# GFNet mixing and an MLP by Winograd doubles: ten plain steps and 31 doubles in place of twelve and 30, and the token sums begun earlier

## The chip, the cores and the metric

The kernel runs on one core of a Trainium2 chip. The metric is the device time of one launch in microseconds (us), the median of several runs.

## The reference, cut to what matters

```python
def _A_ref(x, w_r, w_i):                 # S = 2048 tokens, D = 576
    X = rfft2(x) * (w_r + 1j * w_i)
    return irfft2(X, (S, D))

def _B_ref(x, w1, w2):                   # Dff = 4608
    h = maximum(einsum("bsd,df->bsf", x, w1), 0)
    return einsum("bsf,fd->bsd", h, w2)

h = x + _A_ref(_layernorm(x), w_r, w_i)
out = h + _B_ref(_layernorm(h), w1, w2)  # all float32
```

## The kernel before, in words

The first part does the two-dimensional transform as matmuls, multiplies by the complex weight, transforms back, adds the residual and normalises again. A projection step `j` (function `project`) transposes one tile of 128 normalised tokens and writes it to the token chunk's tile `xc` and to DRAM (`xd`). The rest of the time, from about 150 us on, is the MLP.

Every float32 operand is held as a high part (rounded by ScalarE, "split" and `act`) and a low part (the difference, by VectorE or GpSimd), and each product is three matmuls: high by high, high by low, low by high. The 4608 hidden units are 18 groups of 256, the 2048 tokens are 4 chunks of 512 (of 4 tiles of 128).

The MLP has two kinds of work. A **plain step** (group, chunk) is `mm1` (2 halves of 14 matmuls of 512 columns) and `mm2` (4 token tiles of 12 matmuls of 288 columns, each followed by an add of VectorE onto the residual, L625). Between them stands `relu_split`: ScalarE makes the high part (L631), VectorE the low part (L632). A **double** (group, p) does one group for the two chunks of pair p by the Strassen-Winograd scheme: 7 first products (`l1_prod`, 7 matmuls of 512 columns, L816) and 14 second products (`second` and `prod`, 6 matmuls of 288 columns, L921). It needs sums of the weights (GpSimd makes them, `w1_sums` and `w2_sums`), sums of the hidden values (`piece`), and sums T1 to T4 of the two chunks of tokens. These **token sums** are the same for every group, so they are made once, by `sum_jobs`: for each pair p and tile j the four loads from `xd`, four subtractions (two of VectorE, L678 and L679, two of GpSimd, L680 and L681), the high parts (ScalarE), the low parts (VectorE, L672 for columns and L673 for the 32 leftover rows). They pass through two staging buffers (`stage`) to DRAM (`keep`), and `load_sum` brings them back to the chunks' tiles when a double wants them, since both pairs' sums don't fit beside each other.

The order is written out by hand and each engine runs its queue in that order. SP issues nearly all DMAs in program order. `STEPS` orders the projections with the first plain steps; then a loop over i runs `mm1(i + 1, q)` and `mm2(i, q)` in quarters (i, q), and behind each quarter a job of `sum_jobs`. The last plain step END is woven into the first double's first products. After it each `slot(d)` weaves the first products of double d + 1 with the second products of double d. Slots alternate: one prepares the next group's W1 (its parts A11, S12, S34: `weights`), the other, with `turn` set, prepares A2 and W2 and streams the other pair's sums in (`STREAM`).

All four banks `ps()` of the plain loop's PSUM are handed out in a ring: each `mm1` pair and each `mm2` tile takes the next one, so that TensorE waits when VectorE has not read the bank of three or four pieces before.

Of the kernel before, what the change touches and what calls it, by code (L numbers as in the profile page):

```python
# [129 lines left out]
def kernel(ctx: ExitStack, tc: tile.TileContext, x, w_r, w_i, w1, w2, cc2, c1, fb, ib, c3, out):  # L130
# [518 lines left out]
    def sum_jobs(p, j):  # L649

        fs = FT[j % 2]
        b11, b12, b21, t2, b22 = (fs[k > 1][:, 384 * k - 768 * (k > 1):384 * k - 768 * (k > 1) + 384] for k in range(5))
        v3 = lambda v, a=3: v.rearrange("p (a n) -> p a n", a=a)
# [8 lines left out]

        def high(k):
            f = fs[k][:, :768].rearrange("p (m a n) -> p m a n", m=2, a=3)
            o = stage[k].rearrange("p (m a n) -> p m a n", m=2, a=5)
            for m in range(2):
                act(o[:, m, 0:3], f[:, m])

        def low(k):
            f = fs[k][:, :768].rearrange("p (m a n) -> p m a n", m=2, a=3)  # L670
            o = stage[k].rearrange("p (m a n) -> p m a n", m=2, a=5)
            nc.vector.tensor_sub(o[:, :, 3:5], f[:, :, 0:2], o[:, :, 0:2])  # L672
            nc.vector.tensor_sub(o[64:96, :, 2], f[64:96, :, 2], o[64:96, :, 2])  # L673
            for m, n_ in enumerate((("T1", "T3"), ("T4", "T2"))[k]):
                keep(p, n_, (640 * j, stage[k][:, 640 * m:640 * m + 640]))

        def sums_():
            nc.vector.tensor_sub(b11, b12, b11)  # L678
            nc.vector.tensor_sub(t2, b22, b11)  # L679
            nc.gpsimd.tensor_sub(b12, b22, b12)  # L680
            nc.gpsimd.tensor_sub(b21, b21, t2)  # L681

        def highs():
            high(0)
            high(1)

        def lows():
            low(0)
            low(1)

        return load, sums_, highs, lows
# [475 lines left out]
```

## Time and profile before

| | |
|---|---|
| median of 3 runs | 975.83 us (975.36 to 976.69) |
| the profiled execution's own time | 975.89 us |
| its span | 974.1 us |
| granted TensorE clock, mean | 0.999 |
| TensorE busy | 961.8 us, 99% of the span |
| VectorE, ScalarE, GpSimd busy | 753.8, 454.3, 607.0 us |
| data moved | 178.71 MB, mean 183 GB/s |

The own time is 1.8 us longer than the span, which holds only what the profiler recorded of the engines. Busy time is that of the engines' instructions; TensorE's matmuls are pipelined, so a start-to-start distance says more than a duration of one.

### The profile page before, as it was taken

The page shows a single profiled execution, that of the slowest core. Times are in us where ns is not written, and L with a number is a line of the kernel's source. Part 1 is how long each engine was busy: PE and PEld are TensorE (multiplying, and loading weights), DVE is VectorE, ACT ScalarE, POOL GpSimd, SP SyncE. Part 2 cuts the span into 40 slices and gives each one's busy share as a digit, 9 for nine tenths or more (in the row PEclk, how much of TensorE's full clock was granted, in tenths as well). Part 3 has the DMA queues.
Part 4 walks back from the last instruction along what each step waited for, and adds up shares of the span by engine and source line. Part 5 has one row for each costly group of instructions (what it writes and reads, how often), then busy time and mean ns, then how long its engine had stood idle before and what let it go on. Part 6 is the DMA issues. An engine that isn't in the chain of part 4 may idle for free.

```text
span 974.1 us, 18067 instructions
## 1 busy us (share of the span) xinstructions
PE 961.8 (99%) x6677; PEld 852.9 (88%) x6677; DVE 753.8 (77%) x1190; ACT 454.3 (47%) x887; POOL 607.0 (62%) x740
## 2 busy tenths in 40 slices
PE   8999999999999999999999999999999999999997
PEld 7777678899988899999999999999999999999997
DVE  8677977357665888888888887888887888888886
ACT  6544556223244445445454454444454544544441
POOL 7213756312265777777786868776777868687741
PEclk9999999999999999999999999999999999999999
DMA  7874724647697292735537281927355472819365
GB/s 217 228 178 118 174 96 135 215 146 243 225 345 273 69 313 64 262 125 200 183 142 241 85 299 36 313 63 262 124 201 182 144 251 74 298 36 315 110 209 146
DMA packets 124247, 178.71 MB, mean 183 GB/s; under 512 B 7936, under 2 KB 102784, under 8 KB 124160
## 3 DMA queue, kind: packets, MB, share of 16 engines
q1 hardware_dynamic: 123424, 176.68, 56.0%
q8 instruction: 53, 0.87, 0.4%
q10 hardware_dynamic: 736, 0.89, 0.3%
q14 instruction: 34, 0.28, 0.1%
HBM read 153.15 MB, written 23.07 MB: 181 GB/s over the span
## 4 chain that ended last, share of the span: by engine, by line
PE 92%; DVE 5%; DMA 1%; issue 1%; ACT 0%; SPq 0%; POOL 0%; DVEq 0%; POOLq 0%
PE h L816 34%; PE w L921 33%; PE d L156 23%; DMA B<-t1T 1%; DVE A L519 1%; DVE st L215 1%; PE d L564 1%; DVE st L242 1%; DVE A L931 0%; DVE e L536 0%; DVE e L537 0%; DMA X<-in_A_x_dram 0%; PE w L156 0%; PE h L921 0%; ACT X L159 0%
## 5 line engine op out<-in xcount | busy, mean ns | idle before, releaser
L931 DVE TENSOR_TENSOR A<-A,w 128x576 f32<-128x576 f32 x415 | 308.1, 752 | 81.3 <-PE w L921 68.7
L921 PE MATMUL w<-X,D 128*128 128x288 f32 x1416 | 214.9, 294 | 0.1
L921 PEld LDWEIGHTS w<-X,D 128*128 128x128 f32 x1416 | 202.5, 188 | 10.0 <-DVE A L931 0.3
L816 PE MATMUL h<-B,e 128*128 128x512 f32 x630 | 160.1, 393 | 1.2 <-DVE A L625 0.6
L159 ACT ACTIVATE e<-h 128x512 f32<-128x512 f32 x90 | 53.8, 598 | 181.8 <-PE h L816 181.8
L816 PEld LDWEIGHTS h<-B,e 128*128 128x128 f32 x630 | 113.2, 188 | 21.2 <-DMA B<-t1T 0.9
L353 POOL TENSOR_TENSOR e<-e,e 128x512 fp32r<-128x512 f32 (+3 forms) x62 | 81.2, 1309 | 45.9 <-ACT e L159 45.7
L816 PE MATMUL h<-X,e 128*128 128x512 f32 x420 | 106.5, 393 | 0.0
L635 ACT ACTIVATE e<-e 128x512 f32<-128x512 f32 x90 | 56.9, 632 | 104.2 <-DVE e L874 44.7
L353 POOL TENSOR_TENSOR X<-e,X 128x576 fp32r<-128x576 f32 (+1 forms) x32 | 47.2, 1476 | 71.5 <-ACT X L159 71.5
L816 PEld LDWEIGHTS h<-X,e 128*128 128x128 f32 x420 | 75.5, 188 | 13.0
L159 ACT ACTIVATE e<-e 128x256 fp32r<-128x256 f32 (+4 forms) x162 | 74.5, 489 | 24.7 <-DVE e L678 11.1
L840 POOL TENSOR_TENSOR A<-e 128x256 f32<-128x256 f32 x59 | 46.6, 789 | 27.7 <-DVE X L830 24.6
L830 DVE TENSOR_TENSOR D<-A,D 128x512 fp32r<-128x512 f32 x59 | 61.4, 1041 | 0.9 <-ACT D L159 0.9
L921 PEld LDWEIGHTS w<-X 128*128 128x128 f32 x360 | 53.8, 188 | 5.5 <-issue 0.7
L921 PE MATMUL w<-X 128*128 128x288 f32 x360 | 57.0, 294 | 0.5 <-DVE A L931 0.5
L921 PE MATMUL w<-X,e 128*128 128x288 f32 x348 | 55.2, 294 | 0.0
L156 PE MATMUL d<-e,D 128*128 128x288 f32 x384 | 53.6, 295 | 0.0
L816 PE MATMUL h<-C,e 128*128 128x512 f32 x210 | 53.2, 392 | 0.0
L816 PE MATMUL h<-F,e 128*128 128x512 f32 x210 | 53.2, 392 | 0.0
L156 PEld LDWEIGHTS d<-e,D 128*128 128x128 f32 x384 | 51.9, 188 | 1.3 <-issue 0.4
L842 POOL TENSOR_TENSOR A<-e,A 128x256 f32<-128x256 f32 x59 | 51.4, 871 | 0.8 <-DVE A L838 0.8
(168 smaller groups left out, 1863.2 us busy)
## 6 DMA issues: line engine op xcount, KB each, us to landing
X<-t0T SPq DMA_DIRECT2D x16, 768.0 KB, 8.4
X<-t1T SPq DMA_DIRECT2D x16, 768.0 KB, 8.1
e<-in_B_w_dram SPq DMA_DIRECT2D x18, 576.0 KB, 4.3
e<-in_B_w_dram SPq DMA_DIRECT2D x18, 512.0 KB, 3.8
X<-t0T SPq DMA_DIRECT2D x16, 512.0 KB, 8.6
X<-t1T SPq DMA_DIRECT2D x16, 512.0 KB
B<-t0T SPq DMA_DIRECT2D x8, 768.0 KB
F<-t0T SPq DMA_DIRECT2D x8, 768.0 KB
```

The lines of the kernel that those rows point to most:

```text
L156: nc.tensor.matmul(o, l, r, start=start, stop=stop)
L159: nc.scalar.activation(o, i, AF.Copy, **kw)
L215: nc.vector.bn_stats(st[:, i, h, :], xs[:, t0 + i, 288 * h:288 * h + 288])
L242: nc.vector.bn_stats(first(t)[2][:, h, :], xs[:, t, 288 * h:288 * h + 288])
L353: eng.tensor_sub(l, v, h)
L635: nc.scalar.activation(o, i, AF.Relu)
L816: nc.tensor.matmul(o, a, b, start=bool(first) and n_ == 0, stop=n_ == len(ops) - 1, skip_group_check=not first)
L830: (eng or nc.vector).tensor_sub(f[1], v, f[0])
L840: nc.gpsimd.tensor_sub(s3, p0[:, :256], p0[:, 256:])
L842: nc.gpsimd.tensor_sub(s4, p1_[:, :256], s2)
L921: nc.tensor.matmul(P[tt], l[:, q], r, start=first and n_ == 0, stop=end and n_ == 2, skip_group_check=whole and not first)
L931: nc.vector.tensor_add(xt, xt, P)
```

## The change

There are ten plain steps (groups 0 and 1, and two of group 2) and FIRST is 2: the first double is group 2 for pair 0, and the doubles of groups 3 to 17 follow, 31 in all. The raw weights of group 2 are loaded once, for the plain steps and for the double; before, group 2's were loaded for the plain steps and group 3's for the first double. The first slot now is a `turn` slot, and group 3's W1 is prepared during END (`weights(-1, r)`, with VectorE in GpSimd's place for the low parts).

The token sums are begun during the last projections: loads (=L), subtractions (=S), high (=H) and low parts (=W) stand among the steps, and the rest is dealt by hand over 18 quarters (`JOBS`, quarters (3, 0) to (7, 1)). Their inputs land in a region of the big tile instead of in buffer F. T1 and T4 of pair 0 are written where the doubles read them, and not through `stage`; they are stored to DRAM later, in END (`load_sum(0, "T1", True)`), since the pair's sums are streamed in again later. The low parts are four pairs of instructions of half the size in place of two. A31 stands ahead of B20 in `STEPS`.

```diff
--- before.py
+++ after.py
@@ -582,8 +582,8 @@
...
-    steps = [(0, 0), (0, 1), (0, 2), (1, 1), (0, 3), (1, 3), (1, 0), (1, 2), (2, 3), (2, 1), (2, 0), (2, 2)]
-    FIRST = 3
+    steps = [(0, 0), (0, 1), (0, 2), (1, 1), (0, 3), (1, 3), (1, 0), (1, 2), (2, 3), (2, 2)]
+    FIRST = 2
     END = len(steps) - 1
 
...
+    def sum_jobs(p, j, place):
+
+        part = lambda v, k: v[:, 384 * k:384 * k + 384]
+        i0 = 7680 + 1536 * (j % 2)
+        b11, b21, b12, b22 = (tail[0][:, i0 + 384 * k:i0 + 384 * k + 384].bitcast(F32) for k in range(4))
+        outs, terms, parts = {}, {}, {}
 
         def load():
-            for t, (x, y) in ((8 * p + j, (b11, b21)), (8 * p + 4 + j, (b12, b22))):
-                nc.sync.dma_start(x[:, :256], xd[t][:, :256])
-                nc.sync.dma_start(y[:, :256], xd[t][:, 384:])
-                for h, v in enumerate((x, y)):
-                    o, i = v[:, 256:], xd[t][32 * h:32 * h + 32, 256:384]
-                    nc.sync.dma_start(o, bass.AP(tensor=i.tensor, offset=i.offset, ap=[[0, 4], list(i.ap[0]), [1, 128]]))
+            q = nc.sync
...
+        def sums_():
+            t1, t3, t4, t2 = (part(v, k) for v, k in FT[place])
+            nc.vector.tensor_sub(t1, b12, b11)
+            nc.vector.tensor_sub(t2, b22, t1)
+            nc.gpsimd.tensor_sub(t3, b22, b12)
+            nc.gpsimd.tensor_sub(t4, b21, t2)
+            terms.update(T1=t1, T3=t3, T4=t4, T2=t2)
 
...
+            for m, n_ in enumerate((("T1", "T3"), ("T4", "T2"))[k]):
+                if p == 0 and not m:
+                    hi, lo = (v.rearrange("p a n -> p (a n)").rearrange("p (j a n) -> p j a n", j=4, n=128)[:, j] for v in TF[n_])
+                else:
+                    stage.append(stage.pop(0))
+                    outs[n_] = stage[-1]
+                    o = outs[n_].rearrange("p (a n) -> p a n", a=5)
+                    hi, lo = o[:, :3], o[:, 3:]
+                parts[n_] = hi, lo, terms[n_].rearrange("p (a n) -> p a n", a=3)
+                act(hi, parts[n_][2])
 
...
+            for n_ in (("T1", "T3"), ("T4", "T2"))[k]:
+                hi, lo, v = parts[n_]
+                nc.vector.tensor_sub(lo, v[:, :2], hi[:, :2])
+                nc.vector.tensor_sub(hi[64:96, 2], v[64:96, 2], hi[64:96, 2])
+                if n_ in outs:
+                    keep(p, n_, (640 * j, outs[n_]))
+
+        return dict(L=load, S=sums_, H=lambda: high(0), I=lambda: high(1), W=lambda: low(0), X=lambda: low(1))
 
...
-    def load_sum(p, n):
+    def load_sum(p, n, back=False):
+        if back:
+            td[p, n] = dram.tile([128, 2560], F32, name=f"t{p}{n}")
...
+            nc.sync.dma_start(*((t, v) if back else (v, t)))
 
...
-    doubles = [(g, p) for g in range(FIRST, NG) for p in ((0, 1) if g % 2 == FIRST % 2 else (1, 0))]
+    doubles = [(FIRST, 0)] + [(g, p) for g in range(FIRST + 1, NG) for p in ((1, 0) if g % 2 == FIRST % 2 else (0, 1))]
     LAST = len(doubles) - 1
 
...
-        return [wps[8 - 2 * bank + k][:, :288] for k in range(2)]
+        return [wps[4 + k if bank == 2 else 2 + (k + LAST + 1) % 2][:, :288] for k in range(2)]
 
...
-        g, p = doubles[d]
-        turn = d % 2
-        if not turn and r == 0 and d:
+        g = doubles[max(d, 0)][0]
+        turn = (d + 1) % 2
+        eng = nc.vector if d < 0 else nc.gpsimd
+        if not turn and r == 0 and d > 0:
             w2_split("T34", nc.vector)
             w2_split("B22", nc.gpsimd)
         if g == NG - 1:
@@ -976,20 +980,22 @@
...
             for n_, k in STREAM:
-                if k == r:
+                if max(k, 2 * (d == 0)) == r:
                     load_sum(doubles[d + 2][1], n_)
         else:
+            if r == (1 if d > 0 else 5):
+                load_w2(g + 1, vs[2])
             if r == 1:
-                load_w2(g + 1, vs[2])
-                w1_split("A11", nc.gpsimd)
-            if r == 2:
+                w1_split("A11", eng)
+            early = d < 0
+            if r == 2 - early:
                 w1_sums(0)
-            if r == 3:
+            if r == 3 - early:
                 w1_sums(1)
-            if r == 4:
-                w1_split("S12", nc.gpsimd)
-            if r == 5:
-                w1_split("S34", nc.gpsimd)
+            if r == 4 - early:
+                w1_split("S12", eng)
+            if r == 5 + early:
+                w1_split("S34", eng)
 
...
-        "B12 n14 B13 j12 V0 A20 j13 V1 A21 j14 A30 j15 B20 B21 A31 B22 B23 "
+        "B12 n14 B13 j12 V0 =L0 =L1 A20 j13 V1 =P0 A21 =S0 j14 A30 =S1 j15 =L2 =L3 A31 B20 =P1 B21 =H0 B22 =W0 =H1 B23 =W1 =S2 "
     )
 
...
+        groups.extend(sum_jobs(k // CH, k % CH, v) for k, v in enumerate("ABCABABA"))
+
+    groups, stage, FT = [], [], {}
+
+    def keep_block(p):
+        keep(p, "B22", *((at, v.rearrange("p a n -> p (a n)")) for at, v in zip((0, 1536), khalf(2 * p + 1, 1))))
+
...
+    JOBS = (
+        "L4 / H2 I0 I1 / W2 X0 X1 / S3 L5 I2 / X2 H3 I3 / W3 X3 K1 / S4 L6 / "
+        "H4 I4 / W4 X4 / S5 L7 / H5 I5 / W5 X5 / S6 / H6 I6 / W6 X6 / S7 / H7 I7 / W7 X7"
+    ).split(" / ")
+
...
+    def work(k):
+        for v in JOBS[k].split() if 0 <= k < len(JOBS) else ():
+            job(v[0], int(v[1:]))
 
...
     for i in range(3, END):
         if i == 3:
-            load_weights(2, leftover())
-        if i == 8:
-            vs[1], vs[2], vs[4] = ebuf([128, 4, 256]), ebuf([128, 2, D]), leftover()
-            load_w1(FIRST, vs[1], vs[4])
-            load_w2(FIRST, vs[2])
-        if i == 8:
-            TF.update(T1=khalf(1, 0), B22=khalf(1, 1), T2=khalf(3, 0), T3=khalf(3, 1))
+            TF.update(B22=khalf(1, 1), T2=khalf(3, 0), T3=khalf(3, 1))
         for q in range(4):
             if q < 2:
                 mm1(i + 1, q)
             mm2(i, q)
-            if i == 3 and q == 1:
...
+            if (i, q) == (3, 1):
+                TS = sb([128, 5, 512], "F", dt=F32R)
+                TF["T4"] = TS[:, 0:3], TS[:, 3:5]
+            work(4 * i + q - 12)
+            if (i, q) == (4, 3):
+                load_weights(FIRST, leftover())
+                vs[1], vs[2], vs[4] = raw[FIRST]
+            if (i, q) in ((5, 3), (7, 1)):
+                split_weights(FIRST, i > 5)
+            for n_, k in (("T2", (7, 1)), ("T3", (7, 2))):
                 if k == (i, q):
                     load_sum(doubles[0][1], n_)
...
+            if (i, q) == (END - 2, 2):
...
                 w2_sums()
-            if (i, q) in ((9, 3), (10, 0)):
+            if (i, q) in ((END - 2, 3), (END - 1, 0)):
                 w2_split(("T34", "T12")[q == 3], nc.gpsimd)
...
-                        w1_split(n_, nc.vector if n_ == "A11" else nc.gpsimd)
+                        w1_split(n_, nc.vector if n_ == "A2" else nc.gpsimd)
...
     for i in (END,):
         load_w1(FIRST + 1, vs[1], vs[4])
+        load_sum(0, "T1", True)
...
-            for n_, k in STREAM:
-                if k == r:
-                    load_sum(doubles[1][1], n_)
+            if r == 5:
+                load_sum(0, "T4", True)
+            weights(-1, r)
```

Three places show how the rows move. The first is VectorE behind `mm2(7, 1)`, with the split of group 2's second weight (L353, 128x4x288) that `mm2(8, 0)` reads. The letters are tiles: A the residual, e and F buffers, X the big tile, d a PSUM bank. Before:

```order
L625 TENSOR_TENSOR A_1396<-A_1396,d_3018 128x576
L672 TENSOR_TENSOR e_2463<-F_2541,e_2463 128x2x256
L673 TENSOR_TENSOR e_2463<-F_2541,e_2463 32x2x128
L672 TENSOR_TENSOR e_2464<-F_2541,e_2464 128x2x256
L673 TENSOR_TENSOR e_2464<-F_2541,e_2464 32x2x128
L353 TENSOR_TENSOR X_2146<-e_2474,X_2146 128x4x288
L625 TENSOR_TENSOR A_1396<-A_1396,d_3046 128x576
```

And in the changed kernel (the left-out rows repeat the pair ahead of them):

```order
L625 TENSOR_TENSOR A_1396<-A_1396,d_3090 128x576
L687 TENSOR_TENSOR e_2460<-A_1396,e_2460 128x256
L688 TENSOR_TENSOR e_2460<-A_1396,e_2460 32x128
...
L687 TENSOR_TENSOR e_2461<-e_2339,e_2461 128x256
L688 TENSOR_TENSOR e_2461<-e_2339,e_2461 32x128
...
L353 TENSOR_TENSOR X_2149<-e_2781,X_2149 128x4x288
L625 TENSOR_TENSOR A_1396<-A_1396,d_3120 128x576
```

Four low parts stood ahead of the split, and now eight do (a pair for each of T1 to T4).

The second place is VectorE at the end of the first double and the start of slot 0, up to the add that frees the bank of the first second-product (w, L931). Before:

```order
L874 TENSOR_TENSOR e_3413<-e_3413,h_3476 128x512
L882 TENSOR_TENSOR e_3413<-e_3413,h_3477 128x512
L830 TENSOR_TENSOR X_2146<-e_3413,X_2146 128x256
L836 TENSOR_TENSOR A_1396<-e_3413,e_3501 128x256
L838 TENSOR_TENSOR A_1396<-A_1396,e_3413 128x256
L830 TENSOR_TENSOR D_3479<-A_1396,D_3479 128x512
L353 TENSOR_TENSOR e_3410<-e_3413,e_3617 128x256
L931 TENSOR_TENSOR A_1396<-A_1396,w_3615 128x2x288
```

And now (lines are three higher from `load_sum` on, L934 is the add):

```order
L877 TENSOR_TENSOR e_3229<-e_3229,h_3295 128x512
L885 TENSOR_TENSOR e_3229<-e_3229,h_3296 128x512
L833 TENSOR_TENSOR X_2149<-e_3229,X_2149 128x256
L839 TENSOR_TENSOR A_1396<-e_3229,e_3320 128x256
L841 TENSOR_TENSOR A_1396<-A_1396,e_3229 128x256
L353 TENSOR_TENSOR e_3225<-e_3136,e_3225 128x512
L377 TENSOR_TENSOR e_3227<-e_3229,e_3227 32x256
L833 TENSOR_TENSOR D_3298<-A_1396,D_3298 128x512
L353 TENSOR_TENSOR e_3226<-e_3229,e_3450 128x256
L934 TENSOR_TENSOR A_1396<-A_1396,w_3448 128x2x288
```

The two low parts of group 3's S34 (L353 128x512 and L377) have moved in ahead of the low part of the hidden sums (L833, D) and of the add.

The third place is SP in END, from the load of group 3's W1 on (e and G are raw weights, t0T and t1T the stored sums of pairs 0 and 1). Before:

```order
L333 DMA e_3090<-in_B_w_dram 128x4x256
L335 DMA G_3092<-in_B_w_dram 32x2x256 x3
L706 DMA X_2146<-t1T_3042 128x4x384
L706 DMA X_2146<-t1T_3042 128x4x256
L706 DMA B_1413<-t1T_3034 128x4x384
L706 DMA B_1413<-t1T_3034 128x4x256
```

And now:

```order
L333 DMA e_2780<-in_B_w_dram 128x4x256
L335 DMA G_2778<-in_B_w_dram 32x2x256 x3
L709 DMA t0T_3286<-B_1413 512x1x384
L709 DMA t0T_3286<-B_1413 512x1x256
L709 DMA t0T_3433<-F_2590 512x1x384
L709 DMA t0T_3433<-F_2590 512x1x256
L343 DMA e_2781<-in_B_w_dram 128x2x576
```

The loads of pair 1's T2 and T1 have left this place, since the second double now is of pair 0 too; two sums of pair 0 are stored in their stead.

## Rows read from the trace of the kernel before

**Rows 1.** The page, busy time of each engine.

```profile
PE 961.8 (99%) x6677; PEld 852.9 (88%) x6677; DVE 753.8 (77%) x1190; ACT 454.3 (47%) x887; POOL 607.0 (62%) x740
```

**Rows 2.** Windows of 25 us: busy per engine, clock, DMA share, GB/s.

```profile
core 0: us, PE busy (x) PEld busy (x) DVE busy (x) ACT busy (x) POOL busy (x), PEclk, DMA share, GB/s
...
225.00:250.00 25.00, 25.00 (x151) 22.61 (x149) 17.31 (x28) 9.89 (x17) 5.82 (x6) 1.00 0.58 195
...
275.00:300.00 25.00, 24.36 (x141) 21.66 (x140) 12.04 (x18) 9.61 (x19) 19.51 (x24) 1.00 0.80 292
```

**Rows 3.** Waits of TensorE: engine, line, releaser: us, times, longest.

```profile
PE h L816 <- DVE A L625: 0.6, 1, 0.6
PE h L816 <- DMA B<-t1T: 0.6, 1, 0.6
```

**Rows 4.** Timeline of TensorE, plain steps: start us, us, line, operation.

```profile
186.59 3.38 PE L156 MATMUL d<-X,F 128*128 128x512 f32 x14
...
194.62 4.90 PE L156 MATMUL d<-e,D 128*128 128x288 f32 x36
...
275.92 3.38 PE L156 MATMUL d<-C,e 128*128 128x512 f32 x14
```

**Rows 5.** Chain that ended last, in order of time, two doubles' beginnings.

```profile
806.08 1.62 PE h L816 x7
...
828.42 1.60 PE h L816 x7
```

**Rows 6.** Timeline of TensorE, first double and slot 0.

```profile
289.47 1.85 PE L816 MATMUL h<-B,e 128*128 128x512 f32 x7 [0.64 <-DVE A L625]
...
310.47 1.65 PE L816 MATMUL h<-B,e 128*128 128x512 f32 x6 [0.60 <-DMA B<-t1T]
311.96 1.75 PE L921 MATMUL w<-X,D 128*128 128x288 f32 x12
```

**Rows 7.** Timeline of VectorE, first double and slot 0.

```profile
292.94 0.75 DVE L625 TENSOR_TENSOR A<-A,w 128x576 f32<-128x576 f32 x1 [3.61 <-PE w L156]
299.33 0.76 DVE L625 TENSOR_TENSOR A<-A,w 128x576 f32<-128x576 f32 x1 [5.63 <-PE w L156]
...
309.46 0.43 DVE L838 TENSOR_TENSOR A<-A,e 128x256 f32<-128x256 f32 x1
310.58 0.69 DVE L830 TENSOR_TENSOR D<-A,D 128x512 fp32r<-128x512 f32 x1 [0.70 <-ACT D L159]
311.19 0.42 DVE L353 TENSOR_TENSOR e<-e,e 128x256 fp32r<-128x256 f32 x1
311.53 0.75 DVE L931 TENSOR_TENSOR A<-A,w 128x576 f32<-128x576 f32 x1
```

**Rows 8.** Timeline of VectorE, behind mm2(7, 1).

```profile
248.72 0.69 DVE L672 TENSOR_TENSOR e<-F,e 128x512 fp32r<-128x512 f32 x1
249.42 0.42 DVE L673 TENSOR_TENSOR e<-F,e 32x256 fp32r<-32x256 f32 x1
...
251.02 1.36 DVE L353 TENSOR_TENSOR X<-e,X 128x1152 fp32r<-128x1152 f32 x1
```

**Rows 9.** Timeline of TensorE, first mm2 of step 8.

```profile
253.62 1.74 PE L156 MATMUL d<-X,D 128*128 128x288 f32 x12
```

**Rows 10.** Timelines of VectorE and GpSimd near 282 us.

```profile
282.35 1.57 DVE L673 TENSOR_TENSOR e<-e,e 32x256 fp32r<-32x256 f32 x1
...
282.21 3.01 POOL L353 TENSOR_TENSOR X<-e,X 128x576 fp32r<-128x576 f32 x2 [2.64 <-ACT X L159]
```

**Rows 11.** Timelines of VectorE and ScalarE: a relu's second half; a high part.

```profile
234.16 1.22 DVE L632 SCALAR_TENSOR_TENSOR D<-d,D 128x1024 fp32r<-128x1024 f32 x1 [1.89 <-ACT D L631]
...
241.95 0.53 ACT L159 ACTIVATE e<-F 128x384 fp32r<-128x384 f32 x1 [6.18 <-DMA t0T<-e]
```

**Rows 12.** DMA issues 150 to 330 us; one window of 10 us.

```profile
t1T<-e SPq DMA_DIRECT2D x16, 320.0 KB, 6.7
...
280.00:290.00 10.00, 9.36 (x59) 8.49 (x58) 8.62 (x12) 5.45 (x12) 7.63 (x10) 1.00 1.06 384
```

More of the change, by code (lines that the diff above doesn't have):

```diff
@@ L647, in keep @@
             nc.sync.dma_start(td[p, n][:, at:at + v.shape[1]], v.bitcast(F32))
[L649 to L653, printed above, removed]
-        def load():
-            for t, (x, y) in ((8 * p + j, (b11, b21)), (8 * p + 4 + j, (b12, b22))):
-                nc.sync.dma_start(x[:, :256], xd[t][:, :256])
-                nc.sync.dma_start(y[:, :256], xd[t][:, 384:])
-                for h, v in enumerate((x, y)):
-                    o, i = v[:, 256:], xd[t][32 * h:32 * h + 32, 256:384]
-                    nc.sync.dma_start(o, bass.AP(tensor=i.tensor, offset=i.offset, ap=[[0, 4], list(i.ap[0]), [1, 128]]))
-        def high(k):
[L664 to L667, printed above, removed]
-        def low(k):
[L670 to L691, printed above, removed]
@@ L1055, in tail_in, with sum_bufs, job @@
         load_weights(1, v4)
+        groups.extend(sum_jobs(k // CH, k % CH, v) for k, v in enumerate("ABCABABA"))
+    groups, stage, FT = [], [], {}
+    def keep_block(p):
+        keep(p, "B22", *((at, v.rearrange("p a n -> p (a n)")) for at, v in zip((0, 1536), khalf(2 * p + 1, 1))))
+    def sum_bufs(k):
+        if k == 0:
+            a, b = (ebuf([128, 1152]) for _ in range(2))
+            FT.update(A=((sums, 0), (sums, 1), (a, 0), (a, 1)), B=((b, 0), (b, 1), (b, 2), (a, 2)))
+            TF["T1"] = khalf(1, 0)
+        if k == 1:
+            c = ebuf([128, 1152])
+            FT["C"] = (c, 0), (c, 1), (c, 2), (sb([128, 512], "G"), 0)
+            for _ in range(2):
+                v = ebuf([128, 1280], F32R)
+                stage.extend((v[:, :640], v[:, 640:]))
+    JOBS = (
+        "L4 / H2 I0 I1 / W2 X0 X1 / S3 L5 I2 / X2 H3 I3 / W3 X3 K1 / S4 L6 / "
+        "H4 I4 / W4 X4 / S5 L7 / H5 I5 / W5 X5 / S6 / H6 I6 / W6 X6 / S7 / H7 I7 / W7 X7"
+    ).split(" / ")
+    def job(name, k):
+        if name in "LSHIWX":
+            groups[k][name]()
+        else:
+            dict(K=keep_block, P=sum_bufs)[name](k)
+    def work(k):
+        for v in JOBS[k].split() if 0 <= k < len(JOBS) else ():
+            job(v[0], int(v[1:]))
     CALLS = dict(h=inv_h, d=inv_d, o=inv_o, r=inv_r, e=inv_e, s=stat2, n=lambda t: norm2(t, 2), j=project,
@@ L1060 @@
     for step in STEPS.split():
-        CALLS[step[0]](int(step[1:] or 0))
-    stage = [ebuf([128, 1280], F32R) for _ in range(2)]
-    for p in range(2):
-        keep(p, "B22", *((at, v.rearrange("p a n -> p (a n)")) for at, v in zip((0, 1536), khalf(2 * p + 1, 1))))
-    jobs = []
+        if step[0] == "=":
+            job(step[1], int(step[2:]))
+        else:
+            CALLS[step[0]](int(step[1:] or 0))
     fx = {}
@@ L1103 @@
                 w2_sums()
-            if (i, q) in ((9, 3), (10, 0)):
+            if (i, q) in ((END - 2, 3), (END - 1, 0)):
                 w2_split(("T34", "T12")[q == 3], nc.gpsimd)
-            if i == 10:
+            if i == END - 1:
                 if q == 0:
```

31 lines of the change are left out of this document (9 added, 22 removed), and 2 rows, old and new, of the table STEPS.

## The prediction

> **What bounds the kernel now.** I read the page first: TensorE is busy for 99% of the span and the next engine, VectorE, for 77% [rows 1]. So nearly every microsecond less of matmuls is one less of time, if the other engines keep pace; and what they can lose is little, because they have slack only between the deadlines that TensorE sets. Next the windows of 25 us. In the plain loop (225 to 250 us) TensorE has no idle at all, at a granted clock of 1.00 (the 2.4 GHz level), and VectorE has 7.7 us of 25 free; TensorE's first gap of size lies between 275 and 300 us, 0.64 us [rows 2]. Then the waits: the two long ones in the part that changes are 0.6 us for a VectorE add and 0.6 us for the load of a token sum [rows 3]. The timeline puts the first at the beginning of the first double, where the residual adds of the last plain steps come late (0.64), and the second in slot 0, where T1 of pair 1 has not landed (0.60) [rows 6].
>
> **Two plain steps less, one double more.** The start of a plain step's `mm1` stands at 186.59 and, seven steps later, at 275.92 [rows 4]: 89.33 / 7 = 12.76 us a step, 25.52 for two. A double is seven pairs of pieces, 806.08 to 828.42, with nothing between them: 22.34 us [rows 5]. It does seven eighths of the products of two plain steps, and 25.52 x 7/8 = 22.33 agrees. The exchange is worth 22.34 - 25.52 = **-3.18 us** on TensorE. It holds only where TensorE stays fed, since nothing was idle there before.
>
> **The token sums.** The eight groups of sums are made between the last projections and step 7, where they took steps 3 to 9 before. The low parts are eight instructions a group in place of four, each of half the size. Those of 128x256 take 0.42 us (the L353 row at 311.19) [rows 7]. No row has VectorE at 32x128: above it stands 32x256 at 0.42 [rows 8], below it nothing; I take 0.3, nearer to the row, since halving 128x512 took it only from 0.69 to 0.42. A group then costs 4 x 0.42 + 4 x 0.3 = 2.9 us (1.7 to 3.4) where it cost 2 x (0.69 + 0.42) = 2.2. Eight groups: 5 us more of VectorE, against 7.7 free in each 25. On average that is hidden; what counts is what stands behind the lows in the queue. Two places are tight.
>
> The first is `mm2(8, 0)`. Its third matmul reads the low part of group 2's second weight. Before, that split started at 251.02 and ended at 252.38 [rows 8]; TensorE began at 253.62 and wanted the low part two matmuls of twelve later, at 253.9 [rows 9]. Step 8 keeps its clock time, for what is removed comes later. Now eight lows stand ahead, so the split ends at about 252.38 + 0.66 = 253.0, with 0.9 in hand, if nothing holds it. But right behind it the program has GpSimd's weight sums and the low parts T34, which stood two steps later before. Where these two kinds met, a 32x256 low of VectorE took 1.57 us in place of 0.42, inside a pair of GpSimd lows of 3.01 [rows 10]: 1.15 us lost to one meeting. One meeting puts the split's end at 254.2, a wait of 0.3; both GpSimd lows ahead of it, at 256.0, 2.1. I take **+0.5** (0 to 2.1), nearest to the one meeting that the row shows, with a little for the half-size lows that meet the sums too.
>
> The Trainium skill, page "SBUF — State Buffer", section "Who interferes with whom", speaks against this change: a VectorE instruction with two SBUF inputs shares a read port with a GpSimd instruction that reads SBUF, and whichever comes second is blocked for the whole of the other. The 1.57 beside 0.42 agrees with it. By the row of one meeting the sum has 0.5 here; by the rule taken to its end, two GpSimd lows in front of the split, it would have 2.1, and the total below would be -0.9 in place of -2.5.
>
> The second place is the low part of the relu of step 7. Before, it started at 234.16, after 1.89 us idle, and ended at 235.38 [rows 11]; TensorE wants its bank at 275.92 - 3 x 12.76 = 237.64, so 1.89 + 2.26 = 4.1 us are in hand. The lows of group 5 stand a few rows ahead, 0.7 us longer, and ScalarE's high parts for them wait until the staging buffer's last store has landed; ScalarE waited so for a store before as well (6.18 us idle in front of a high part) [rows 11]. A store lands 6.7 us after its issue, in the median for pair 1 [rows 12]. I take **+0.1** (0 to 1.5).
>
> **END and slot 0.** The wait of 0.64 at the beginning of the first double stays: the same adds of the last `mm2` release it. Inside END VectorE takes over low parts of A2, A11 and S12 (0.69 + 0.42, 0.42, 0.69 + 0.42 by the same shapes): they fit into gaps of 3.61 and 5.63 us [rows 7], nothing on the path. SP loads group 3's W1 at the beginning of END, as it did before, and two stores of sums replace two loads of as many bytes. In slot 0 the wait for T1 goes (-0.60), as the second double uses the same pair's sums. But S34's low parts (0.69 + 0.42 = 1.11) now stand in front of the hidden sums' low part and of the add that frees the bank of the third second-product. Before, the instruction ahead of them ended at 309.89 and 0.70 of idle followed [rows 7]. Now: lows to 311.00, then the same starts 0.61 and 0.34 apart, the add from 311.95 to 312.70. Without the T1 wait TensorE gets to that product at 311.96 - 0.60 + half of the twelve matmuls (0.8) = 312.2 [rows 6]. It waits 0.5 to 0.9, I take 0.7: net **+0.1** (-0.6 to +0.3).
>
> **At nothing.** The raw weights that are no longer loaded twice and the doubled region in the big tile: DMAs that no row of TensorE waited for. The exchange of A11 and A2 between VectorE and GpSimd in the last plain step but END: the same number of low parts on either side, behind adds with idle after them. The last slots are unchanged but for the order of two banks.
>
> **The sum.** -3.18 + 0.5 + 0.1 + 0.1 = -2.5 us. On the profiled execution's own 975.89 that is 973.4; the median of the runs is 0.06 lower, too little to matter. A measurement of this kernel can tell about 0.2%, 1.95 us, from no change: the line is 973.9. So the forecast lies on the fast side of it by half a microsecond.
>
> **Rivals.**
> - All is hidden, and the T1 wait goes too: -3.18 - 0.60 = -3.8, **972.1**. For it: VectorE has a third of its time free [rows 2]. Against: the queue order in front of the two deadlines. 0.18.
> - VectorE and GpSimd block each other, not once but through the whole run of lows: `mm2(8, 0)` waits 2.1, the relu's low part behind it 0.6, slot 0 as above: -3.18 + 2.1 + 0.6 + 0.1 = -0.4, **975.5**, no change that can be told. For it: the weight sums and T34 now need VectorE's busiest quarter. Against: GpSimd can also have finished before, as its inputs are long there. The Trainium skill's rule on the shared port, named above, would make it so if GpSimd comes first each time. 0.28.
> - Slower, by the staging buffers: stores of pair 1's sums queue on SP behind the 1.28 MB block of pair 1, the loads of the next group and group 2's weights; the high parts wait for them, and behind these on ScalarE the relu, for which VectorE and then TensorE wait. The 4.1 us in hand are used up first; slower by over 0.2% begins when TensorE's waits pass 3.18 + 1.95 = 5.1, that is with a store 9.2 us late. With 9 or 10 us late twice it is **978** and more. For it: 384 GB/s moved for 10 us near 285 us, at a DMA share of 1.06 [rows 12], so queues do fill. Against: over 225 to 250 us it was 195 GB/s [rows 2]. 0.10.
> - The forecast, waits of 0.2 to 1.2 in all: 0.44.
>
> **The numbers.** Faster: the forecast, the first rival, less a little of the forecast's upper edge: 0.60. Within 0.2%: 0.30. Slower: 0.10. The forecast's own range is 972.4 to 973.9; the range for 8 in 10 runs from just under the first rival, 971.9, to 977.0, over the second rival with one more late store.
>
> **What would show it.** Right: plain steps still 12.76 apart up to step 7, the first double about 25.5 earlier than 289.47, 31 doubles of 22.34, no wait for T1, a wait for the split (L353, VectorE) at the beginning of `mm2(8, 0)` under 1 us, one for the add in slot 0 of 0.5 to 0.9. Wrong: a `mm1` that waits for L632, or ScalarE idle on a store in front of a relu (the third rival); or a chain of GpSimd lows in front of the split (the second). A plain step or a double of another length would overthrow the first term, and with it all.

## The result and the profile after

The changed kernel takes 980.58 us (median of 6 runs, 979.13 to 981.97) against 975.70 (6 runs, 975.34 to 976.69): ratio 1.0050, 95% interval 1.0037 to 1.0063. It is 4.9 us slower; the forecast was 2.5 faster. The profiled execution took 979.13 (span 977.2), the quickest of the six.

The page, against [rows 1]:

```profile
PE 958.8 (98%) x6658; PEld 849.8 (87%) x6658; DVE 778.1 (80%) x1244; ACT 464.6 (48%) x912; POOL 628.5 (64%) x764
```

TensorE has 3.0 us less to do, as the first term of the sum said, and the span is 3.1 longer: 6 us of new idle. Waits of TensorE, against [rows 3]:

```profile
PE d L156 <- DVE X L353: 3.6, 1, 3.6
PE w L924 <- DVE A L934: 1.9, 2, 1.4
PE d L156 <- DVE A L625: 0.7, 1, 0.7
PE d L156 <- DVE D L632: 0.3, 1, 0.3
```

Windows of 25 us, against [rows 2]: between 250 and 275 us, where TensorE was full before, it now has 4.2 us idle. Before:

```profile
250.00:275.00 25.00, 25.00 (x151) 22.61 (x150) 16.47 (x26) 6.15 (x10) 6.08 (x6) 1.00 0.83 265
```

And now:

```profile
225.00:250.00 25.00, 23.93 (x138) 21.12 (x137) 16.54 (x32) 11.23 (x20) 7.51 (x9) 1.00 0.60 219
250.00:275.00 25.00, 20.79 (x122) 18.44 (x121) 17.62 (x21) 6.15 (x14) 15.54 (x17) 1.00 0.57 197
275.00:300.00 25.00, 23.55 (x134) 20.84 (x134) 17.33 (x27) 12.31 (x25) 15.30 (x19) 1.00 0.39 128
```

The timeline of TensorE gives the place of each, against [rows 4, 6, 9]:

```profile
224.74 3.38 PE L156 MATMUL d<-C,X 128*128 128x512 f32 x14
...
236.80 1.85 PE L156 MATMUL d<-e,D 128*128 128x288 f32 x12 [0.72 <-DVE A L625]
239.00 3.49 PE L156 MATMUL d<-X,e 128*128 128x512 f32 x14 [0.35 <-DVE D L632]
...
251.87 3.38 PE L156 MATMUL d<-C,e 128*128 128x512 f32 x14
255.09 0.42 PE L156 MATMUL d<-X,D 128*128 128x288 f32 x2
259.09 1.59 PE L156 MATMUL d<-X,D 128*128 128x288 f32 x10 [3.58 <-DVE X L353]
...
269.25 1.85 PE L819 MATMUL h<-B,e 128*128 128x512 f32 x7 [0.64 <-DVE A L625]
...
286.88 1.75 PE L819 MATMUL h<-B,e 128*128 128x512 f32 x7
...
293.34 1.03 PE L924 MATMUL w<-X,D 128*128 128x288 f32 x6 [1.45 <-DVE A L934]
...
311.26 1.78 PE L819 MATMUL h<-C,e 128*128 128x512 f32 x7
```

From start to start, which counts the restart behind a stop (0.15 to 0.27) with it: the `mm1` at 224.74 stands 0.14 earlier than before, which is no more than executions differ by: in the traces of all versions of the changed kernel it starts between 224.48 and 225.16. The step from there takes 14.26 in place of 12.76 (+1.50), the next 12.87 (+0.11), the last before END 17.38 (251.87 to 269.25) in place of 13.55 (+3.83). The first double with END takes 17.63 as before, slot 0 24.38 in place of 23.51 (+0.87). With -3.18 for the exchange that is +2.99; the last matmul starts 2.97 later (971.81 against 968.84).

What VectorE does behind `mm2(7, 1)`, against [rows 8]: eight low parts of group 7 (L687, L688), then the split for which TensorE waits 3.58 us.

```profile
250.19 1.59 DVE L687 TENSOR_TENSOR e<-A,e 128x256 fp32r<-128x256 f32 x1
251.79 1.43 DVE L688 TENSOR_TENSOR e<-A,e 32x128 fp32r<-32x128 f32 x1
253.25 0.85 DVE L687 TENSOR_TENSOR e<-A,e 128x256 fp32r<-128x256 f32 x1
254.12 0.73 DVE L688 TENSOR_TENSOR e<-A,e 32x128 fp32r<-32x128 f32 x1
...
257.53 1.50 DVE L353 TENSOR_TENSOR X<-e,X 128x1152 fp32r<-128x1152 f32 x1
```

GpSimd over the same time, against [rows 10]: the low parts of T34 and T12 (sums of the first double's second weight), then the eight sums of its first weight, the W1 sums (L742 to L745).

```profile
250.06 3.02 POOL L353 TENSOR_TENSOR X<-e,X 128x576 fp32r<-128x576 f32 x2 [0.69 <-ACT X L159]
253.04 0.78 POOL L742 TENSOR_TENSOR e<-e 128x256 f32<-128x256 f32 x1
253.90 0.80 POOL L743 TENSOR_TENSOR e<-e,e 128x256 f32<-128x256 f32 x1
...
257.78 1.57 POOL L745 TENSOR_TENSOR e<-G,e 128x128 f32<-128x128 f32 x1
```

VectorE's starts follow GpSimd's one by one: 253.25 and 253.04, 254.12 and 253.90, and so on. Undisturbed, the same low parts take 0.42 and 0.28 (217.65 and 218.08 in the same trace). It costs the other side too: GpSimd's last W1 sum, beside the split, takes 1.57 where the same shape takes 0.46 later (280.37). The run of eight lasts 7.3 us (250.19 to 257.53).

### The profile page after: what moved, and what is told of

It is laid out like the page before. It is cut to its first block, busy times and chain, and to the rows that moved or that the text cites. A ratio compares the mean times of both kernels' runs of the same rounds, so it can differ in the third digit from the quotient of the medians.

```text
span 977.2 us, 18090 instructions
## 1 busy us (share of the span) xinstructions
PE 958.8 (98%) x6658; PEld 849.8 (87%) x6658; DVE 778.1 (80%) x1244; ACT 464.6 (48%) x912; POOL 628.5 (64%) x764
## 4 chain that ended last, share of the span: by engine, by line
PE 87%; DVE 7%; issue 2%; DMA 2%; ACT 1%; SPq 0%; POOL 0%; DVEq 0%; POOLq 0%; ACTq 0%
PE h L819 35%; PE w L924 34%; PE d L156 16%; DVE A L519 1%; DMA e<-in_B_w_dram 1%; DVE st L215 1%; PE w L156 1%; DVE A L625 1%; PE d L564 1%; DVE st L242 1%; DVE A L934 1%; DVE e L687 1%; DMA t1T<-e 1%; DVE e L536 0%; DVE e L537 0%
## 5 line engine op out<-in xcount | busy, mean ns | idle before, releaser
L934 DVE TENSOR_TENSOR A<-A,w 128x576 f32<-128x576 f32 x429 | 318.1, 751 | 85.2 <-PE w L924 72.2
L924 PE MATMUL w<-X,D 128*128 128x288 f32 x1464 | 222.4, 294 | 1.5 <-DVE A L934 1.4
L924 PEld LDWEIGHTS w<-X,D 128*128 128x128 f32 x1464 | 209.4, 188 | 11.9 <-ACT e L635 1.7
L819 PE MATMUL h<-B,e 128*128 128x512 f32 x658 | 166.9, 393 | 0.6 <-DVE A L625 0.6
L819 PEld LDWEIGHTS h<-B,e 128*128 128x128 f32 x658 | 118.3, 188 | 21.2 <-issue 0.8
L353 POOL TENSOR_TENSOR e<-e,e 128x512 fp32r<-128x512 f32 (+3 forms) x63 | 82.7, 1312 | 52.2 <-ACT e L159 52.1
L819 PE MATMUL h<-X,e 128*128 128x512 f32 x434 | 110.0, 392 | 0.0
L635 ACT ACTIVATE e<-e 128x512 f32<-128x512 f32 x93 | 58.8, 633 | 107.0 <-DVE e L877 45.6
L353 POOL TENSOR_TENSOR X<-e,X 128x576 fp32r<-128x576 f32 (+1 forms) x34 | 50.1, 1474 | 69.6 <-ACT X L159 69.6
L819 PEld LDWEIGHTS h<-X,e 128*128 128x128 f32 x434 | 78.0, 188 | 13.4
L159 ACT ACTIVATE e<-e 128x256 fp32r<-128x256 f32 (+5 forms) x171 | 78.7, 489 | 12.3 <-DVE e L666 6.1
L833 DVE TENSOR_TENSOR D<-A,D 128x512 fp32r<-128x512 f32 x61 | 62.5, 1024 | 0.0
L845 POOL TENSOR_TENSOR A<-e,A 128x256 f32<-128x256 f32 x61 | 53.6, 879 | 0.8 <-DVE A L841 0.8
```

The lines of the kernel that those rows point to most:

```text
L159: nc.scalar.activation(o, i, AF.Copy, **kw)
L353: eng.tensor_sub(l, v, h)
L635: nc.scalar.activation(o, i, AF.Relu)
L819: nc.tensor.matmul(o, a, b, start=bool(first) and n_ == 0, stop=n_ == len(ops) - 1, skip_group_check=not first)
L833: (eng or nc.vector).tensor_sub(f[1], v, f[0])
L845: nc.gpsimd.tensor_sub(s4, p1_[:, :256], s2)
```

## The experiments

Theory A: VectorE's low parts lose time to each GpSimd instruction that runs beside them, and the split behind them comes late. Theory B: eight low parts are simply too many in front of the split, whatever GpSimd does. For the other losses, which can stand beside either: stores that come late in SP's queue, and S34's low parts in slot 0.

**e1_split_first.** The split of W2 (group 2's second weight) ahead of group 7's low parts.

```diff
+            if (i, q) == (7, 1):
+                split_weights(FIRST, 1)
             work(4 * i + q - 12)
...
-            if (i, q) in ((5, 3), (7, 1)):
-                split_weights(FIRST, i > 5)
+            if (i, q) == (5, 3):
+                split_weights(FIRST, 0)
```

> The split of group 2's second weight stands ahead of the eight low parts of group 7 behind mm2(7, 1), nothing else changes. Theory A (VectorE and GpSimd block each other behind that quarter): the split needs at most one meeting, ends before 253, and the wait of 3.6 us at mm2(8, 0) is gone; the lows still take 0.7 to 1.6 us each, only later, and the adds behind them hold up TensorE by 0 to 2 us at the next tiles. Time 1.5 to 3.5 us under the changed kernel. Theory B (eight lows are too many before the split, whatever GpSimd does): the same wait goes, the lows take 0.42 and 0.28, and nothing is given back: 3.5 us or more.

Measured: 976.18 us (975.25 to 976.51, 10 runs), ratio 1.0001 (0.9992 to 1.0011). No wait for the split is left, though it is held up itself (2.52 us from 250.43, 1.36 undisturbed). One moved line gives back 4.4 us in the median, more than the 1.5 to 3.5 of theory A; by the time alone theory B would have it. The low parts decide against B: behind the split they are still held up, the eight taking 6.6 us (252.87 to 259.43), and the last step before END now takes 13.82, 0.27 over the kernel before. Between the two profiled executions the gain is only 2.96 (979.13 and 976.17); e9 shows what the medians hold beyond that.

**e2_memset.** GpSimd writes zeros where it made the low parts of T34 and T12 and the W1 sums of the first double.

```diff
-                w2_split(("T34", "T12")[q == 3], nc.gpsimd)
+                n_ = ("T34", "T12")[q == 3]
+                k = 576 * (n_ == "T34")
+                act(W2[n_][0], v2d(vs["s"][:, k:k + 576]))
+                nc.gpsimd.memset(W2[n_][1].bitcast(F32), 0.0)
...
-                    w1_sums(0)
+                    for k in range(4):
+                        nc.gpsimd.memset(vs["s"][:, 256 * k:256 * k + 256], 0.0)
...
-                    w1_sums(1)
+                    for v in vs["r"]:
+                        nc.gpsimd.memset(v, 0.0)
```

> The low parts of T34 and T12 and the sums of W1 of the first double (ten GpSimd subtractions of 128x576 to 128x128) are replaced by GpSimd memsets of the same regions, so that part of the first double's weights is zero; VectorE, ScalarE and the order are unchanged. Theory A (the reads of the two engines exclude each other): memsets read nothing, so the lows of group 7 take 0.42 and 0.28 us again, the split ends near 255, the wait of 3.6 us falls under 0.5, and the time is about 3.5 us under the changed kernel. Theory B (eight lows started late): lows and wait stay, time unchanged.

Measured: 975.20 us (974.54 to 976.20, 10 runs), ratio 0.9996 (0.9987 to 1.0005). VectorE at the same place:

```profile
249.75 0.42 DVE L687 TENSOR_TENSOR e<-A,e 128x256 fp32r<-128x256 f32 x1
250.18 0.28 DVE L688 TENSOR_TENSOR e<-A,e 32x128 fp32r<-32x128 f32 x1
...
252.76 1.36 DVE L353 TENSOR_TENSOR X<-e,X 128x1152 fp32r<-128x1152 f32 x1
```

GpSimd beside them:

```profile
249.88 1.08 POOL L1137 MEMSET e<- 128x256 f32 x4
```

The order of VectorE's instructions is the same, and GpSimd is busy beside the first lows here too, but only writes: every low part takes its undisturbed time, the eight 3.0 us, and the wait of 3.58 is gone. Theory A holds and B falls: what costs is GpSimd's reading, not its being busy. GpSimd's writes are over sooner than the work that they replace (248.84 to 251.69, against 250.06 to 259.35), so only the first five lows show it.

**e3_block_late.** The store of pair 1's block (K1) six quarters later.

```diff
-X2 H3 I3 / W3 X3 K1 / S4 L6 / H4 I4 / W4 X4 / S5 L7 / H5 I5 / W5 X5 / S6
+X2 H3 I3 / W3 X3 / S4 L6 / H4 I4 / W4 X4 / S5 L7 / H5 I5 / W5 X5 K1 / S6
```

> The store of pair 1's block of 1.28 MB (K1) goes from the sixth quarter of the table to the twelfth, behind the stores of group 5. Theory C (group 4's stores queue behind that block and the weights, and ScalarE waits for them): the idle of 8.9 us in front of the high part of group 5 shrinks by 3 us or more, the waits of 0.7 and 0.4 us in step 6 go, and the time falls by 1.0 to 1.7 us. If the block has no part in it, step 6 stays at 14.3 us.

Measured: 980.13 us (979.32 to 980.35, 5 runs), ratio 1.0040 (1.0026 to 1.0054). The step from 224.74 takes 13.73 in place of 14.26, and ScalarE still waits 8.32 for a store of group 4 (8.88 in the changed kernel), 0.56 less where 3 or more was forecast. The block is about a third of that step's loss (0.53 of 1.50); the other stop stays at 3.56.

**e4_s34_late.** S34's low parts to GpSimd, behind slot 0's first sums.

```diff
-            if r == 5 + early:
+            if r == 5 and not early:
                 w1_split("S34", eng)
...
+            if late and r == 0:
+                w1_split("S34", nc.gpsimd)
             weights(d, r)
```

> The low parts of group 3's S34 leave VectorE's queue in front of slot 0's first add and go to GpSimd behind the hidden sums of that quarter. If they make the wait of 1.45 us for the add, it falls to 0.3 or less and the time by 1.0 to 1.7 us; if the wait comes from GpSimd's reads in that place (it then has 2 us more of them), it stays over 1 us.

Measured: 981.76 us (980.72 to 982.33, 4 runs), ratio 1.0057 (1.0042 to 1.0072). In slot 0 the stop of 1.45 becomes one of 0.62, now for ScalarE (L635), and a new one of 0.34 for GpSimd's L353. From its start to its end slot 0 is only 0.18 shorter (24.20), and the 1.0 to 1.7 us that were forecast did not come. The whole time can't size this edit: behind the stop of 3.56 us TensorE's granted clock was 0.50 for 6 us (258 to 264) in the profiled execution.

**e5_queue_order.** e1, K1 late as in e3, and group 2's raw weights loaded behind group 4's stores.

```diff
-            if (i, q) == (4, 3):
+            if (i, q) == (5, 0):
                 load_weights(FIRST, leftover())
```

> Three queue orders at once: the split ahead of group 7's lows, the block's store (K1) behind the stores of group 5, and the load of group 2's weights behind the stores of group 4 (one quarter later). If the stores of group 4 wait for what stands ahead of them on SP, the idle of 8.3 us in front of group 5's high part shrinks to 5 or less and step 6 takes 12.8 to 13.1 us; the time is 974.5 to 975.5, so 0.7 to 1.7 under e1. If the weights, loaded later, now hold up the split of W1, step 6 stays at 13.7 or more and the time near 976.

Measured: 974.42 us (974.16 to 975.20, 11 runs) against 975.69, ratio 0.9987 (0.9978 to 0.9996). In the changed kernel SP issues the weights first, and group 4's stores (t1T) behind them:

```profile
220.44 0.75 SPq L333 DMA_DIRECT2D e<-in_B_w_dram  x1
221.29 1.57 SPq L335 DMA_DIRECT2D G<-in_B_w_dram  x3
222.90 0.43 SPq L343 DMA_DIRECT2D e<-in_B_w_dram  x1
223.44 4.19 SPq L647 DMA_DIRECT2D t1T<-e  x4
```

and ScalarE waits for them:

```profile
230.10 0.53 ACT L159 ACTIVATE e<-A 128x384 fp32r<-128x384 f32 x1 [8.88 <-DMA t1T<-e]
```

In e5 the stores go first, and ScalarE starts 5 us earlier:

```profile
219.71 2.86 SPq L647 DMA_DIRECT2D t1T<-e  x4
222.61 0.73 SPq L333 DMA_DIRECT2D e<-in_B_w_dram  x1
```

```profile
225.14 0.53 ACT L159 ACTIVATE e<-A 128x384 fp32r<-128x384 f32 x1 [3.83 <-DMA t1T<-e]
```

That step takes 12.77 (224.82 to 237.59), with no stop. Against e1, where it took 14.11 (225.16 to 239.27), 1.8 us are gained in the median: 1.34 here. Another 0.34 in the trace is the step's start, which lies within the spread of executions. No run moves the weights alone; e3 has K1 alone.

**e6_s34_halves.** e5, with S34's low parts in two halves behind the first add of slot 0.

```diff
+            if late and r in (0, 2):
+                k = r // 2
+                a, b = slice(256 * k, 256 * k + 256), slice(128 * k, 128 * k + 128)
+                nc.vector.tensor_sub(W1["S34"][1][:, a], vs["s"][:, 512:1024][:, a], W1["S34"][0][:, a])
...
```

> As e5, and the low parts of S34 are taken in halves on VectorE: S3's behind the first add of slot 0, S4's two products later. What stood in front of the first add is gone, and no GpSimd work is added: the wait of 1.45 us falls to about 0.6 (what e4 had left), the next adds come 0.7 later, which costs 0 to 0.5. Time 0.3 to 0.8 under e5, at best 973.9.

Measured: 974.98 us (974.12 to 975.15, 11 runs), ratio 0.9988 (0.9979 to 0.9996), 0.56 slower than e5 where 0.3 to 0.8 faster was forecast. The stop of 1.40 became three, 0.58, 0.38 and 0.43 (at 287.58, 290.59 and 297.68), and slot 0 takes 25.32 in place of e5's 24.60.

**e7_lows_on_gpsimd.** The changed kernel with group 7's eight low parts on GpSimd, and nothing else.

```diff
-                nc.vector.tensor_sub(lo, v[:, :2], hi[:, :2])
-                nc.vector.tensor_sub(hi[64:96, 2], v[64:96, 2], hi[64:96, 2])
+                eng = nc.gpsimd if (p, j) == (1, CH - 1) else nc.vector
+                eng.tensor_sub(lo, v[:, :2], hi[:, :2])
+                eng.tensor_sub(hi[64:96, 2], v[64:96, 2], hi[64:96, 2])
```

> The changed kernel, but the eight low parts of the last group (7) are done by GpSimd in its own order, ahead of its weight sums: nothing that VectorE does behind mm2(7, 1) but the split has two SBUF inputs. Theory A: the two engines meet once or twice, the split ends before 253, the wait of 3.6 us is gone; GpSimd is 5 us later with T34, T12 and the sums of W1, and slower in what follows, which can cost 0 to 2 us at the beginning of the first double. Time 976 to 978.5. Under theory B (too much work for VectorE behind that quarter) it would be the same number, so here the lows' own times tell: GpSimd's 128x256 at 0.74, and no VectorE row over its usual 1.36 by more than one GpSimd instruction.

Measured: 975.12 us (974.75 to 976.37, 10 runs), ratio 0.9996 (0.9987 to 1.0006), better than the 976 to 978.5 that were forecast: GpSimd starts its W1 sums 5.7 us later (258.73), and no new stop of TensorE comes of it. On the engine that they had met, the lows take 0.75 and 0.46 (one 1.92, beside the split), and the split starts at 250.19, takes 1.35, and no one waits for it; the stops of the step before (0.66 and 0.35) and of slot 0 (1.44) stay.

**e8_sums_late.** The W1 sums behind A11's low part on GpSimd, so that the lows meet T34 and T12 only.

```diff
-                if q == 0:
-                    w1_sums(0)
...
-                    w1_sums(1)
                 if q:
                     for n_ in (("A11",), ("S12",), ("S34", "A2"))[q - 1]:
                         w1_split(n_, nc.vector if n_ == "A2" else nc.gpsimd)
+                if q == 1:
+                    w1_sums(0)
+                    w1_sums(1)
```

> The changed kernel with GpSimd's W1 sums of the first double (L742 to L745, eight instructions, 4.9 us) issued behind the low part of A11 instead of behind those of T34 and T12, so that group 7's eight low parts on VectorE meet only the two low parts of T34 and T12 (3.0 us). It sizes what each set of GpSimd instructions takes from the eight lows, which lasted 7.3 us. Theory A (each VectorE low that falls beside a GpSimd instruction is held up by it, and so the W1 sums carry more than half of the loss): the two first lows stay at about 1.5 us each, the other six fall to 0.4 and 0.3, the split of W2 starts near 255.5 and takes 1.4, mm2(8,0) waits about 1.4 us instead of 3.6; the kernel gains 2 us or more, 978.5 (977 to 979.5), less if the first slot then waits for the W1 sums, which are 5 to 8 us later. Rival (the two T lows alone hold the lows up): the wait stays at 3 us or more and the kernel at 980 to 982.

Measured: 978.03 us (977.55 to 978.55, 10 runs), ratio 1.0025 (1.0016 to 1.0034). VectorE:

```profile
250.24 1.58 DVE L687 TENSOR_TENSOR e<-A,e 128x256 fp32r<-128x256 f32 x1
251.84 1.43 DVE L688 TENSOR_TENSOR e<-A,e 32x128 fp32r<-32x128 f32 x1
253.30 0.42 DVE L687 TENSOR_TENSOR e<-A,e 128x256 fp32r<-128x256 f32 x1
253.74 0.28 DVE L688 TENSOR_TENSOR e<-A,e 32x128 fp32r<-32x128 f32 x1
...
255.56 1.36 DVE L353 TENSOR_TENSOR X<-e,X 128x1152 fp32r<-128x1152 f32 x1
```

TensorE behind it:

```profile
256.97 1.58 PE L156 MATMUL d<-X,D 128*128 128x288 f32 x10 [1.41 <-DVE X L353]
```

This splits the loss. The eight lows last 3.0 us alone (e2), 5.3 with T34 and T12 (250.24 to 255.56), 7.3 with the W1 sums as well: 2.3 and 2.0 us. The wait of 1.41 is what the theory gave; the rival (3 or more) falls. In END a new stop of 0.53 appears, for a high part of ScalarE, so the kernel did not gain all of it.

**e9_unchanged.** The changed kernel once more, for a second profile.

> The changed kernel itself, once more, for one further profile of the stretch behind the stop of 3.6 us. If TensorE's granted clock falls behind that stop in most executions and not in the one profiled so far: a window of 2 us just behind it shows about 0.5, the execution takes 980 to 982 and its last matmul starts 1 to 3 us later than 971.8. If the clock has no part in the spread of 979.1 to 982: 1.00 there again, and whatever time it takes over 979.1 lies elsewhere.

Measured: 980.84 us (one run). Windows of 2 us (granted clock third from the right), the first profile of the changed kernel:

```profile
258.00:260.00 2.00, 0.91 (x7) 0.91 (x8) 2.00 (x3) 0.00 (x0) 1.35 (x1) 1.00 0.75 239
260.00:262.00 2.00, 2.00 (x13) 1.74 (x12) 1.11 (x2) 0.00 (x0) 0.00 (x0) 1.00 0.93 327
```

and this one:

```profile
258.00:260.00 2.00, 0.91 (x5) 0.91 (x6) 2.00 (x3) 0.00 (x0) 1.35 (x1) 0.88 0.76 233
260.00:262.00 2.00, 2.00 (x9) 1.90 (x8) 0.80 (x2) 0.00 (x0) 0.00 (x0) 0.50 0.89 311
262.00:264.00 2.00, 2.00 (x8) 1.55 (x8) 0.32 (x1) 0.00 (x0) 0.00 (x0) 0.77 1.07 361
```

Behind the same stop (3.58 us there, 3.56 here) the clock fell to half, the 1.2 GHz level, and the last matmul started at 973.45 in place of 971.81: 1.64 later, of the 1.71 between the two times. The first double already starts 1.61 later (270.86 against 269.25), so nearly all of it is lost there.

**e10_queue_s34.** e5 and e4's edit together.

> The version of the earlier run with the split of W2 first and the stores and weights exchanged on SyncE (974.4), and the low parts of S34 on GpSimd behind the first slot's first sums, which with the other stops in place had turned one wait of 1.45 us into one of 0.62 and a new one of 0.34. If the first slot's stops add up as they stand in the trace (each with 0.2 of restart): 974.0 (973.6 to 974.5), 0.3 to 0.5 under that version. Rival (the first slot's end is set by the sums that VectorE and GpSimd have to do in it, whatever their order): 974.3 to 975.

Measured: 974.21 us (973.64 to 974.44, 11 runs) against 975.59, ratio 0.9983 (0.9974 to 0.9992): 1.4 us faster than the kernel before, and not to be told from e5 by these intervals. The timeline of TensorE:

```profile
263.99 1.84 PE L819 MATMUL h<-B,e 128*128 128x512 f32 x7 [0.64 <-DVE A L625]
...
287.51 1.03 PE L924 MATMUL w<-X,D 128*128 128x288 f32 x6 [0.57 <-ACT e L635]
...
292.57 1.42 PE L819 MATMUL h<-X,e 128*128 128x512 f32 x5 [0.39 <-POOL e L353]
```

The first double starts 25.48 earlier than before [rows 6], as forecast (25.5). Slot 0 still takes 24.49 (281.59 to 306.08), 0.11 less than in e5. The time lies within the first forecast's range, but only 0.21 under e5 where 0.3 to 0.5 was forecast, so it does not decide between the two; the length of the slot speaks for the rival.

## Why the prediction was wrong

Between the forecast and the medians lie 7.4 us. The traces of the two profiled executions show 5.5 of them: 3.3 at `mm2(8, 0)`, 1.5 at the relu of step 7, 0.8 in slot 0, less 0.1 at the start. About 1.6 more is the clock, by e9.

**The exchange, -3.18: right.** TensorE's busy time is 3.0 lower, plain steps stand 12.76 apart up to the one at 224.74 (186.46 and three steps), a double takes 22.32 (805.88 to 828.20 in the chain). With the stops ahead of it taken away, e10 has the first double where the sum put it.

**`mm2(8, 0)`, +0.5 with 2.1 as the upper bound: the step that failed.** The place, the instruction waited for and the mechanism were right; the price was not, and its bound was no bound. "One meeting" was taken as the likely case and "both GpSimd lows ahead of it" as the worst. Measured: 3.58 of idle, 3.83 from start to start. The first two lows lose 2.3 us to T34 and T12; with that alone the wait is 1.41 (e8), inside the bound. But GpSimd does not stop there: its next waiting instruction is A11's low part, so it runs on into eight W1 sums, and each low that is left loses 0.14 to 0.45 to them, 2.0 in all. The prediction did name these sums, but gave them only "a little" of its 0.5: it counted the instructions next to the lows and not all that GpSimd could reach. Its argument that GpSimd may have finished before did not hold either: T34 and T12 waited for ScalarE's high part and started at 250.06, 0.13 ahead of the first low. The 0.9 in hand was right: with e2's 3.01 and 1.36 the split would end at 254.56, and TensorE wants it at 255.51 (255.09 + 0.42).

The Trainium skill, page "SBUF — State Buffer", section "Who interferes with whom", was weighed and discounted: it has a VectorE instruction with two SBUF inputs fully blocked by a GpSimd instruction that reads SBUF, and not by one that only writes. Both halves agree with the runs: 1.59 and 0.85 in place of 0.42 beside reading instructions, 0.42 beside the memsets of e2. For two instructions of GpSimd the 0.5 was too small and the 2.1, the rule taken to its end, held: e8 has 1.41. The error was to stop at two and not to apply the rule to the whole queue of GpSimd.

**A term that was missing: the clock.** Past its first instruction TensorE's longest wait before was 0.7 us, with the clock at 1.00 in the windows of [rows 2], so the sum had no term for it. In the profiled execution of the changed kernel the clock costs nothing, in e9 1.64 us. The profiled executions before and after differ by 3.24 (975.89 and 979.13); with 1.64 that is 4.88, the difference of the medians. So close a match is chance, since the 1.64 comes from one pair of executions; but the mean granted clocks of the whole executions point the same way: 0.996 to 0.998 in the six of the changed kernel, 0.999 to 1.000 in the ten of e1, without the stop.

**The relu of step 7, +0.1 (0 to 1.5): too small, 1.50 and 0.11 behind it.** (The expectations call the step that lost this time step 6.) The chain is the third rival's in small: stores behind loads on SP, ScalarE's high parts waiting for them, VectorE's lows and the add (L625) behind these. The term asked how long a store takes and not when it is issued; the queue on SP, group 2's weights among it, stood only in the third rival, and there for losses over 5.1 us. (That rival's sum is loose: by its own terms one store 9 or 10 us late gives about 978, and two give 982 or more.) Group 4's stores stand behind five DMAs of raw weights that the change moved in front of them. e5 changes the order and the loss is gone; e3 shows that the block of pair 1 alone is about a third of it.

**Slot 0, +0.1 (-0.6 to +0.3): too small, 0.87.** The wait for T1 has gone, as said. The wait for the add came to 1.45 where 0.5 to 0.9 was forecast:

```profile
289.91 0.69 DVE L353 TENSOR_TENSOR e<-e,e 128x512 fp32r<-128x512 f32 x1
290.62 0.84 DVE L377 TENSOR_TENSOR e<-e,e 32x256 fp32r<-32x256 f32 x1
...
292.44 0.75 DVE L934 TENSOR_TENSOR A<-A,w 128x576 f32<-128x576 f32 x1
```

S34's second low part took 0.84 and not 0.42. But e4, e6 and e10 moved these low parts elsewhere, and stops of 1.0 to 1.4 in all stayed, for ScalarE, GpSimd or VectorE in turn (0.62 for ScalarE in e4, about what T1's 0.60 was). And in e3 and e5, where the low parts stand as in the changed kernel, the same stop (1.40) is put down to ScalarE (L635) and not to the add. So S34 is not the reason for all of it. One loss does not even stand among the waits of the matmuls: in e5 and e10 the weight loads of slot 0's first second-product wait 0.25 and 0.30 us for a low part of GpSimd (L353, X), and the product takes 1.14 and 1.18 from start to start in place of 0.87. What sets the length of this slot stays open.

**The rivals.** The second (VectorE and GpSimd block each other through the whole run of lows) is what happened, at 3.8 us instead of 2.1, with part of the third on top. The failed step is thus a size, and the prediction held the right mechanism in two rivals and took a small price for it.

## What to carry to other kernels

When a run of short VectorE instructions is placed beside GpSimd, count all that GpSimd can reach before its next wait, not just the instructions that the program puts next to it: here ten of them turned 3.0 us into 7.3. What TensorE waits for goes ahead of such a run (e1: one moved split, 4.4 us in the median), and stores that free a buffer go ahead of loads that nobody wants yet. A saving of 3 us on an engine that is 99% busy needs every deadline behind it looked at with the queue's order, since a single missed one took all of it.

## What the runs showed of the hardware

A stop of 3.56 to 3.58 us on TensorE was followed by the 1.2 GHz level in three profiles of four (granted clock 0.50 to 0.52 in the lowest window of 2 us of e3, e4 and e9, 1.00 throughout in the first), with the program the same up to there in e4 and e9. What decides whether it comes stays open. Ten matmuls of 288 columns then took 2.44 to 2.77 us in place of 1.59. The stop of 1.45 us in slot 0 was followed by 1.00 (275 to 300 us). The Trainium skill, page "TensorE: Matmul & The Clock Gate", part 1, has a table of two states of the clock, half and full, and says that the count of slow matmuls at the start of a kernel varies from run to run. The two levels agree with the windows here; that the slow matmuls behind a stop in the middle of a kernel vary too is shown by these four profiles, and the page's sentence does not speak of it.
